# An attention and GEGLU block on Trainium2: pairs on alternating banks and longer blocks in the first max pass

## The chip, the cores and the metric

The kernel runs on one core of one Trainium2 chip. TensorE (PE) does the matrix products into PSUM, VectorE (DVE) the reductions and part of the evictions, ScalarE (ACT) the exponentials and the other evictions, GpSimd (POOL) elementwise work between tiles in SBUF, and SyncE (SP) issues most transfers. The metric is the device time of one execution in microseconds (us).

## The reference

The input x has 2048 rows of 576. After a layer norm, two branches are computed and joined:

```python
xn = layernorm(x)
qkv = (xn @ wqkv)            # 32 heads of 18
p = softmax(q @ k.T * 18 ** -0.5)
s = (p @ v) @ wo
h = gelu(xn @ w_gate) * (xn @ w_up)      # 4608 columns
g = silu(h @ w_down)
out = x + s * g
```

## The kernel before, in words

Each float32 matrix is split into two float16 parts (hi and lo), and a product is three float16 products. The heads are worked on in 16 passes of two heads, each of 64 blocks. For a pass the kernel first needs the maximum of each score row: `qk1` computes a block of 128 x 512 scores of both heads into a tile s1 or s2, and VectorE reduces it to PM (L1218, L1221). Later `qk2` computes the transposed scores, already less the maximum, and ScalarE takes the exponential (L1270, L1276). `max_end` turns the maxima of a pass into two rows of QT.

In the main loop (15 passes) the max blocks of the next pass run beside the exponential blocks of this one. For the first pass (p = 0) there is nothing before, so its 64 max blocks stand alone, filled with other work of TensorE: first the values (`unit_v`, 16 x 2 units of 14 matmuls, evicted by ScalarE to vst and stored to VS), then the stream of *pairs*. Five steps follow, with the first four max blocks of pass 1 and the transposition of the maxima; after them the main loop begins.

The pairs are the projections of the remaining heads (units j1 to j4, four pairs each) and the gate and up products of the 18 chunks c0 to c17 of 256 hidden columns (eight pairs each). A pair fills two PSUM tiles at once: `Pair.slot` issues two matmuls on 64 rows each, one for each tile. A pair has 27 slots, 14 in the first half and 13 in the second, where the two row halves change tiles; between the halves a small VectorE copy (`touch`, L414) orders them. The tiles are `MTile("ma")` and `MTile("mb")`. At the end of a j pair, `evac_j` empties them: evh by ScalarE (L490), evl by VectorE (L495), then six stores to KD and QD on SP (L510). At the end of a c pair, gs and gv are copied by ScalarE (L609, L620), GpSimd and ScalarE compute the gelu and split the result into hhi and hlo, and the down product (`down`, `DownPair`, L730) is queued in `dnq`. `g_run(n)` issues up to n slots of the stream; a half that has ended lets the next begin only with another block.

In the main loop `make_plan` deals the slots that are left (`gs.left`) over the blocks that are left, with the stages of the down pairs (12 matmuls each) and with bursts of the products with the values (L1311), which use md, ma or mb.

The weights of a unit are prepared by the pieces of `prep`: load, a maximum of each of five parts (L234) and of the two parts of the down weights (L239), exchange of the maxima through DRAM, power of two, split into hi (ScalarE) and lo (GpSimd). `subtick` moves the queue of these pieces and of deferred steps on by one tick, as far as its room of time for each engine allows. The tile raw has one buffer, so a load waits for the split of the unit before. The order of the units is v, j1, c0, c1, j2 and so on, and a unit's weights are started two units ahead.

Of the kernel before, what the change touches and what calls it, by code (L numbers as in the profile page):

```python
# [12 lines left out]
F32 = mybir.dt.float32  # L13
# [7 lines left out]
P = 128  # L21
# [12 lines left out]
FIRST = {"A": 0.75, "V": 0.75, "T": 1.3}  # L34
# [53 lines left out]
def on_dve(t=0.7):  # L88
    return {"V": t}
# [7 lines left out]
def kernel(ctx: ExitStack, tc: tile.TileContext, x, wqkv, wo, w_gate, w_up, w_down, out):  # L97
# [33 lines left out]
    defer = Deferred()  # L131
# [60 lines left out]
    class W:  # L192
        pass

    def prep(name, parts, n, down=None, urgent=False, free=None, dfree=None, lead=1, slow=1):


        w = W()
        w.ready = False
        w.n = n  # L200
        pieces = []
        gap = 0 if urgent else 1
# [135 lines left out]
        def fin():  # L338
            w.ready = True

        def add(fn, cost=None):
# [7 lines left out]
        low_cost = dve if urgent else on_pool(2.75)  # L349
        pieces += [(None, None)] * (lead * gap)  # L350
        add(load)
        rest(5 * slow)
        for t in range(5):
            add(lambda t=t: amax(t), dve)
        if down is not None:
# [41 lines left out]
    def half_terms(w, i, cs, xs, half, more):  # L397
# [9 lines left out]
            terms.append((w.lo[r, 4, i, cs], (XT, XU)[half][r, xs]))  # L407
        return terms

    def touch(ap):  # L410

        t = sm.tile([1, 2], F32, tag="touch", name="touch", bufs=2)
        o = t[:, 0:1] if len(ap.shape) == 2 else t.rearrange("p (a b) -> p a b", a=2)
        nc.vector.tensor_copy(o, ap)  # L414

    class Pair:
# [8 lines left out]
        def begin(self):  # L425
            w, ia, ib, cs, xs = self.args
            n = cs.stop - cs.start
            if self.stage == 0:
                self.a = MTile("ma", [P, 512], F32, self.end.readers)
                self.b = MTile("mb", [P, 512], F32, self.end.readers)  # L430
            a, b = self.a.t[0:n], self.b.t[0:n]
            more = self.stage == 0
            self.q = [
                ((a, b)[half ^ self.stage], half_terms(w, (ia, ib)[half ^ self.stage], cs, xs, half, more))
                for half in range(2)
            ]
            self.k = 0
            self.slots = len(self.q[0][1])
# [160 lines left out]
    def gu(w, c, sb, ft):  # L599

        st = {}
        gp = nc.gpsimd
        k = glu["n"]
        glu["n"] += 1

        def end(g, u):
            until(lambda: glu["cubic"] == k)
            st["g"] = wp.tile([P, 512], F32, tag="gs", name=f"gs_{c}_{sb}_{ft}", bufs=1)
            nc.scalar.activation(st["g"], g.t, AF.Copy, scale=w.uE[:, 0:1])  # L609
            g.done()  # L610
            defer.at(defer.now + 1, lambda: up(u), on_act())

        end.readers = 1

        def up(u):
            if glu["low"] < k - 1:
                defer.at(defer.now + 1, lambda: up(u), on_act())
                return
            st["v"] = wp.tile([P, 512], F32, tag="gv", name=f"gv_{c}_{sb}_{ft}")
            nc.scalar.activation(st["v"], u.t, AF.Copy, scale=w.uE[:, 1:2])  # L620
            u.done()
            defer.at(defer.now + 1, cubic)

        def cubic():
            if glu["hp"] < k:
                defer.at(defer.now + 1, cubic)
                return
            glu["cubic"] += 1
            defer.at(defer.now + 2, th, on_act())
            defer.spend(on_pool(4.2))  # L630
            st["t"] = wp.tile([P, 512], F32, tag="tw", name=f"tw_{c}_{sb}_{ft}", bufs=1)
            gp.tensor_tensor(st["t"], st["g"], st["g"], op=ALU.mult)  # L632
            gp.tensor_scalar(st["t"], st["t"], GC, 1.0, op0=ALU.mult, op1=ALU.add)
            gp.tensor_tensor(st["t"], st["t"], st["g"], op=ALU.mult)
            gp.tensor_tensor(st["v"], st["v"], st["g"], op=ALU.mult)

        def th():
            nc.scalar.activation(st["t"], st["t"], AF.Tanh, scale=GK)  # L638
            defer.at(defer.now + 1, hp)
            defer.at(defer.now + 2, hhi, on_act())  # L640

        def hp():
            glu["hp"] += 1
            defer.spend(on_pool(1.9))
            gp.tensor_scalar(st["t"], st["t"], 1.0, 1.0, op0=ALU.mult, op1=ALU.add)  # L645
            gp.tensor_tensor(st["v"], st["v"], st["t"], op=ALU.mult)

        def hhi():
            if ft == 0:
                if not all(k[0] < c - 1 or v.left == 0 for k, v in list(hstate.items())[:-1]):  # L650
                    defer.at(defer.now + 1, hhi, on_act())
                    return
                hs = hstate[c, sb] = W()
                hs.left = 8
                hs.hi = wp.tile([P, 2, 512], F16, tag="hhi", name=f"hhi_{c}_{sb}")
                hs.lo = wp.tile([P, 2, 512], F16, tag="hlo", name=f"hlo_{c}_{sb}")
            elif (c, sb) not in hstate:
                defer.at(defer.now + 1, hhi, on_act())
                return
            nc.scalar.activation(hstate[c, sb].hi[:, ft], st["v"], AF.Copy)  # L660
            defer.at(defer.now + 1, hlo)

        def hlo():
            glu["low"] += 1
            hs = hstate[c, sb]
            defer.spend(on_pool(1.2))
            gp.tensor_tensor(hs.lo[:, ft], st["v"], hs.hi[:, ft], op=ALU.subtract)  # L667
            if ft == 1:
                defer.at(defer.now + 1, lambda: dnq.extend(
                    (w, c, sb, si, hf) for si in range(4) for hf in range(2)  # L670
                ))

        return Pair(w, 0, 1, slice(P * ft, P * ft + P), slice(512 * sb, 512 * sb + 512), end)

    dnq = deque()
# [753 lines left out]
    load_v(0)  # L1429
    stage.open("b")  # L1430
    steps = max_end(0)
# [264 lines left out]
```

## Time and profile before

| | |
|---|---|
| median of 3 runs | 2632.76 us (2630.01 to 2633.9) |
| profiled execution | 2633.47 us, span 2631.7 us |
| granted TensorE clock, mean | 0.991 |
| first max block's reduction begins | 88.48 us |
| first exponential's scores begin | 213.71 us |
| TensorE busy | 2539.2 us |

All times inside the profile count from the start of the span. A row of the timeline has its start, its duration, the engine, the line and the operation with its shapes, and in brackets how long the engine was idle before it and what released it. A matmul's own duration (377 ns for 512 columns) is longer than the distance to the next one, since matmuls are pipelined and two on 64 rows each run side by side.

### The profile page before, as it was taken

What the parts mean: (1) busy time and instruction counts of PE and PEld (TensorE: products, weight loads), DVE (VectorE), ACT (ScalarE), POOL (GpSimd) and SP (SyncE); (2) the same over time, 40 slices, a digit from 0 to 9 for tenths busy, and PEclk for the clock granted to TensorE, in tenths of its full rate; (3) what the DMA queues carried; (4) which work ended last, traced back from release to release, by engine and by line L of the source; (5) the groups of instructions that cost most, each with busy time, mean ns of one, the idle gap of its engine ahead of it and who ended that gap; (6) DMA issues with size and microseconds to landing.
All of it is one profiled execution on the core that took longest, in us unless ns stands there. A gap on an engine that the chain in (4) does not pass through costs nothing.

```text
span 2631.7 us, 59621 instructions
## 1 busy us (share of the span) xinstructions
PE 2539.2 (96%) x25232; PEld 1316.7 (50%) x25232; DVE 1945.6 (74%) x2720; ACT 1660.8 (63%) x2083; POOL 1491.2 (57%) x1422
## 2 busy tenths in 40 slices
PE   6979999999999999999999999999999999999898
PEld 5554445445554545344545554555455555454344
DVE  7676777777787777777877777787778877777444
ACT  5216666666677666666666666777666666666563
POOL 4236654476437554567576666757576665756301
PEclk9989999999999999999999999999999999999999
DMA  4430111201130112111011111102010101100123
GB/s 144 138 90 22 29 44 31 81 18 28 45 94 12 28 38 60 36 39 54 12 43 20 37 25 39 44 22 56 9 51 15 40 23 39 49 9 11 35 77 117
DMA packets 133640, 118.61 MB, mean 45 GB/s; under 512 B 60160, under 2 KB 112792, under 8 KB 133372
## 3 DMA queue, kind: packets, MB, share of 16 engines
q1 hardware_dynamic: 127740, 103.02, 14.9%
q0 software_dynamic: 3072, 8.90, 1.0%
q8 instruction: 197, 3.23, 0.6%
q10 hardware_dynamic: 2560, 2.89, 0.3%
q14 instruction: 71, 0.58, 0.1%
HBM read 84.89 MB, written 29.61 MB: 44 GB/s over the span
## 4 chain that ended last, share of the span: by engine, by line
PE 82%; DVE 8%; ACT 4%; issue 3%; DMA 2%; POOL 1%; SPq 0%; ACTq 0%; DVEq 0%
PE mb_t L444 16%; PE ma_t L444 15%; PE md_t L730 14%; PE s L1270 8%; PE md_t L1311 8%; PE s L1218 8%; PE ma_t L1311 6%; DVE PM L1221 3%; PE pv L1292 1%; PE mc_t L463 1%; ACT P L1276 1%; PE mb_t L1311 1%; DMA obr<-rd 1%; DVE m_c L234 1%; PE mb_t L463 1%
## 5 line engine op out<-in xcount | busy, mean ns | idle before, releaser
L1221 DVE TENSOR_REDUCE PM<-s 128x2 f32<-128x1024 f32 x1024 | 1252.5, 1224 | 345.0 <-PE s L1218 337.0
L1276 ACT ACTIVATE P<-s,etab 128x1024 f32<-128x1024 f32 x896 | 996.7, 1112 | 615.8 <-PE s L1270 604.3
L444 PE MATMUL ma_t<-XHT,whi_c 64*128 64x512 f16 x1440 | 543.2, 377 | 9.5 <-ACT gs L609 5.1
L444 PE MATMUL mb_t<-XHT,whi_c 64*128 64x512 f16 x1440 | 543.0, 377 | 5.7 <-ACT gv L620 2.3
L444 PE MATMUL ma_t<-XHT,wlo_c 64*128 64x512 f16 x1296 | 488.7, 377 | 0.0
L444 PE MATMUL ma_t<-XL,whi_c 64*128 64x512 f16 x1152 | 434.5, 377 | 0.0
L444 PE MATMUL mb_t<-XL,whi_c 64*128 64x512 f16 x1152 | 434.3, 377 | 0.0
L444 PE MATMUL mb_t<-XHT,wlo_c 64*128 64x512 f16 x1152 | 434.3, 377 | 0.0
L1218 PE MATMUL s<-KT,QT 54*128 54x512 f16 x2048 | 404.6, 379 | 15.1 <-DVE PM L1221 10.1
L1270 PE MATMUL s<-QT,KT 56*128 56x512 f16 x2048 | 403.0, 380 | 7.8 <-ACT P L1276 3.1
L444 PEld LDWEIGHTS <-whi_c 64*128 64x128 f16 x5184 | 278.1, 94 | 250.3 <-issue 35.9
L730 PE MATMUL md_t<-dhi_c,hhi 64*128 64x288 f16 x2224 | 330.8, 283 | 1.6 <-DVE touch L414 1.2
L730 PE MATMUL md_t<-dhi_c,hlo 64*128 64x288 f16 x2224 | 330.5, 282 | 0.0
L730 PE MATMUL md_t<-dlo_c,hhi 64*128 64x288 f16 x2224 | 330.0, 282 | 0.0
L645 POOL TENSOR_SCALAR tw<-tw 128x512 f32<-128x512 f32 x144 | 90.4, 628 | 413.5 <-ACT tw L638 413.2
L730 PEld LDWEIGHTS <-hhi 64*128 64x128 f16 x4448 | 239.4, 94 | 130.7 <-issue 13.0
L667 POOL TENSOR_TENSOR hlo<-gv,hhi 128x512 f16<-128x512 f32 x144 | 168.7, 1172 | 214.8 <-ACT hhi L660 209.9
L1311 PE MATMUL md_t<-P,VT 128*32 128x512 f32 x2232 | 262.1, 597 | 0.3
L1270 PEld LDWEIGHTS <-KT 56*128 56x128 f16 x2048 | 124.1, 94 | 260.7 <-issue 173.5
L632 POOL TENSOR_TENSOR tw<-gs 128x512 f32<-128x512 f32 x144 | 152.0, 1055 | 172.7 <-ACT gs L609 172.4
L750 DVE SCALAR_TENSOR_TENSOR y<-md_t,c_c,y 128x576 f32<-128x576 f32 x262 | 211.1, 806 | 1.3 <-PE md_t L730 1.3
L444 PEld LDWEIGHTS <-wlo_c 64*128 64x128 f16 x2592 | 141.2, 94 | 119.4 <-issue 2.0
(262 smaller groups left out, 4098.1 us busy)
## 6 DMA issues: line engine op xcount, KB each, us to landing
draw_c<-in_B_w_down SPq DMA_DIRECT2D x18, 576.0 KB
raw_c<-in_B_w_gate SPq DMA_DIRECT2D x18, 512.0 KB
raw_c<-in_B_w_up SPq DMA_DIRECT2D x18, 512.0 KB
obr<-rd SPq DMA_DIRECT2D x30, 256.0 KB
KT<-KD SPq DMA_DIRECT2D x32, 224.0 KB
QT<-QD SPq DMA_DIRECT2D x32, 216.0 KB
VS<-vst POOLq DMA_DIRECT2D x16, 304.0 KB, 4.0
VT<-VS SPq DMA_DIRECT2D x16, 304.0 KB
```

Of the source, the lines that this page charges most:

```text
L444: nc.tensor.matmul(o, lw, xx, start=self.stage == 0 and self.k == 0, stop=self.stage == 1 and self.k == self.slots - 1, skip_group_check=True,
L463: nc.tensor.matmul(o, xx(t), ww[:, t, i, :], start=(k == 0), stop=False)
L632: gp.tensor_tensor(st["t"], st["g"], st["g"], op=ALU.mult)
L645: gp.tensor_scalar(st["t"], st["t"], 1.0, 1.0, op0=ALU.mult, op1=ALU.add)
L667: gp.tensor_tensor(hs.lo[:, ft], st["v"], hs.hi[:, ft], op=ALU.subtract)
L730: nc.tensor.matmul(self.t.t[:, hf, 0:288], a[r, ft, sl], b[r, ft, 288 * hf:288 * hf + 288], start=self.stage == 0 and k == 0, stop=self.st ...
L750: nc.vector.scalar_tensor_tensor(yy, y, w.c, yy, op0=ALU.mult, op1=ALU.add)
L1218: nc.tensor.matmul(s1[:, h], QT[p][r, P * qt:P * qt + P], KT[p][r, 512 * kb:512 * kb + 512], start=True, stop=True)
L1221: nc.vector.tensor_reduce(PM[p][:, :, qt, kb:kb + 1], s1, op=ALU.max, axis=AX.X)
L1270: nc.tensor.matmul(s2[:, h], KT[p][r, P * kt:P * kt + P], QT[p][r, 512 * qb:512 * qb + 512], start=True, stop=True)
L1276: nc.scalar.activation(pt, s2, AF.Exp, scale=ETAB[j0])
L1311: nc.tensor.matmul(t.t[qd:qd + 32, :], VT[p][:, c0:c0 + 32], pt[:, h], start=kt == k0, stop=kt == k1, skip_group_check=True,)
```

## The change

In the first max pass:

- While the values last, two max blocks are issued back to back, with twice the filling behind them.
- Behind the values, `g_run(7)` instead of `g_run(5)`, and a second, smaller `subtick` for each block.
- The pairs alternate between the banks ma, mb and the banks mc, pv, up to block 56; from there and in the main loop only ma, mb.

And in the preparation: a unit is `ready` before its down weights are split, with a flag `dready` of its own for these, on which the queueing of downs waits; c0's pieces rest 7 ticks behind the load instead of 10.

```diff
-    def prep(name, parts, n, down=None, urgent=False, free=None, dfree=None, lead=1, slow=1):
+    def prep(name, parts, n, down=None, urgent=False, free=None, dfree=None, lead=1, slow=0):
...
-        rest(5 * slow)
+        rest(5 + slow)
...
+            add(fin)
             pieces.append(Gate(dfree))
             add(lambda: dsplit_hi(0), act)
             add(lambda: dsplit_hi(1), act)
             add(lambda: dsplit_lo(0), on_pool(3.0))
             add(lambda: dsplit_lo(1), on_pool(3.0))
-        add(fin)
+            add(dfin)
+        else:
+            add(fin)
...
+    banks = deque([("ma", "mb")])
...
-                self.a = MTile("ma", [P, 512], F32, self.end.readers)
-                self.b = MTile("mb", [P, 512], F32, self.end.readers)
+                ta, tb = banks[0]
+                banks.rotate()
+                self.a = MTile(ta, [P, 512], F32, self.end.readers)
+                self.b = MTile(tb, [P, 512], F32, self.end.readers)
...
+        def queue():
+            if not w.dready:
+                defer.at(defer.now + 1, queue)
+                return
+            dnq.extend((w, c, sb, si, hf) for si in range(4) for hf in range(2))
...
-                lead=8 if i == 3 else 1, slow=2 if i == 2 else 1,
+                lead=8 if i == 3 else 1, slow=2 if i == 2 else 0,
...
-    for k in range(64):
+    k = 0
+    while k < 64:
         if k == 12:
             load_qk(1)
-        qk1(0, k)
-        subtick(FIRST)
         if done_units[0]:
-            g_run(5)
+            if k < 56 and len(banks) == 1:
+                banks.append(("mc", "pv"))
+            elif k >= 56 and len(banks) == 2:
+                banks.remove(("mc", "pv"))
+            qk1(0, k)
+            subtick(FIRST)
+            g_run(7)
+            subtick({"A": 0.75, "V": 0.3, "T": 0.5})
+            k += 1
         else:
-            fill(0.95)
+            qk1(0, k)
+            qk1(0, k + 1)
+            subtick(FIRST)
+            subtick(FIRST)
+            fill(1.9)
+            k += 2
```

What this moves is shown at three places; a name such as s_0_46 is the tile of max block 46 of pass 0, and a number behind it is only the tile's own. On TensorE, the end of the first pair of j1 and the start of the second stand so before:

```order
L444 MATMUL mb_t<-XHT,whi_j_1358 126x512
L444 LDWEIGHTS whi_j_1358
L444 MATMUL ma_t<-XHT,whi_j_1358 126x512
L1218 LDWEIGHTS QT_1074
L1218 MATMUL s_0_46_1980<-KT_1075,QT_1074 128x512 [waits DVE_49]
L1218 LDWEIGHTS QT_1074
L1218 MATMUL s_0_46_1980<-KT_1075,QT_1074 128x512
L444 LDWEIGHTS whi_j_1358
L444 MATMUL ma_t<-XHT,whi_j_1358 126x512 [waits DVE_49]
L444 LDWEIGHTS whi_j_1358
L444 MATMUL mb_t<-XHT,whi_j_1358 126x512 [waits DVE_49]
```

and so in the changed kernel:

```order
L454 MATMUL mb_t<-XHT,whi_j_1349 126x512
L454 LDWEIGHTS whi_j_1349
L454 MATMUL ma_t<-XHT,whi_j_1349 126x512
L1232 LDWEIGHTS QT_1074
L1232 MATMUL s_0_44_1979<-KT_1075,QT_1074 128x512 [waits DVE_49]
L1232 LDWEIGHTS QT_1074
L1232 MATMUL s_0_44_1979<-KT_1075,QT_1074 128x512
L454 LDWEIGHTS whi_j_1349
L454 MATMUL mc_t<-XHT,whi_j_1349 126x512 [waits Activation_49]
L454 LDWEIGHTS whi_j_1349
L454 MATMUL pv_t<-XHT,whi_j_1349 126x512 [waits Activation_49]
```

The second pair begins two blocks earlier, and on banks that the values used last instead of those of the first pair. On VectorE, the maxima of c1's weights stand before among the max blocks of pass 1:

```order
L1221 TENSOR_REDUCE PM_1080<-s_0_63_2275 128x2 [waits PE_49]
L495 SCALAR_TENSOR_TENSOR evl_1_3_2294<-ma_t,evh_1_3_2292 126x512 [waits DMAHW5_49,DVE_49,Activation_49]
...
L414 COPY touch<-mb_t 1x1 [waits PE_49]
L1221 TENSOR_REDUCE PM_1469<-s_1_2_2433 128x2 [waits PE_49]
L234 TENSOR_REDUCE m_c_2442<-raw_c_2279 128x1 [waits DMAHW6_49,DMAHW4_49]
```

and in the changed kernel in block 56 of pass 0:

```order
L505 SCALAR_TENSOR_TENSOR evl_1_3_2262<-mc_t,evh_1_3_2260 126x512 [waits DMAHW5_49,DVE_49,Activation_49]
L505 SCALAR_TENSOR_TENSOR evl_0_3_2266<-pv_t,evh_0_3_2264 126x512 [waits DMAHW7_49,Activation_49]
L1235 TENSOR_REDUCE PM_1080<-s_0_56_2268 128x2 [waits PE_49]
L234 TENSOR_REDUCE m_c_2275<-raw_c_2203 128x1 [waits DMAHW6_49,DMAHW4_49]
L1235 TENSOR_REDUCE PM_1080<-s_0_57_2297 128x2 [waits PE_49]
L234 TENSOR_REDUCE m_c_2275<-raw_c_2203 128x1
L422 COPY touch<-mb_t 1x1 [waits PE_49]
```

The maxima now stand ahead of a touch and of seven of the 64 reductions, behind the fourth j1 pair's evl. On SP, behind the third j1 pair's stores (evl_0_2 is its last), before:

```order
L510 DMA QD_1879<-evl_0_2_2199 7x18x512
L215 DMA raw_c_2279<-in_B_w_gate 128x4x256
L219 DMA raw_c_2279<-in_B_w_gate 128x1x256
L215 DMA raw_c_2279<-in_B_w_up 128x4x256
L219 DMA raw_c_2279<-in_B_w_up 128x1x256
L227 DMA draw_c_2284<-in_B_w_down 128x2x576
L1210 DMA VT_2296<-VS 128x16x38
L510 DMA KD_1880<-evh_1_3_2292 7x18x512
```

and in the changed kernel:

```order
L520 DMA QD_1882<-evl_0_2_2171 7x18x512
L215 DMA raw_c_2203<-in_B_w_gate 128x4x256
L219 DMA raw_c_2203<-in_B_w_gate 128x1x256
L215 DMA raw_c_2203<-in_B_w_up 128x4x256
L219 DMA raw_c_2203<-in_B_w_up 128x1x256
L227 DMA draw_c_2208<-in_B_w_down 128x2x576
L520 DMA KD_1883<-evh_1_3_2260 7x18x512
```

c1's load keeps its place between the third pair's stores and the fourth's; only the transfer of VT goes from before to behind the fourth pair's stores.

More of the change, by code (lines that the diff above doesn't have):

```diff
@@ L193 @@
         pass
-    def prep(name, parts, n, down=None, urgent=False, free=None, dfree=None, lead=1, slow=1):
+    def prep(name, parts, n, down=None, urgent=False, free=None, dfree=None, lead=1, slow=0):
         w = W()
-        w.ready = False
+        w.ready = w.dready = False
         w.n = n
@@ L339, in fin, with dfin @@
             w.ready = True
+        def dfin():
+            w.dready = True
         def add(fn, cost=None):
@@ L668, in hlo @@
             if ft == 1:
-                defer.at(defer.now + 1, lambda: dnq.extend(
-                    (w, c, sb, si, hf) for si in range(4) for hf in range(2)
-                ))
+                defer.at(defer.now + 1, queue)
+        def queue():
+            if not w.dready:
+                defer.at(defer.now + 1, queue)
+                return
+            dnq.extend((w, c, sb, si, hf) for si in range(4) for hf in range(2))
         return Pair(w, 0, 1, slice(P * ft, P * ft + P), slice(512 * sb, 512 * sb + 512), end)
```

## The prediction

> **What bounds the kernel now.** I began with the page's busy shares and its chain, to learn which engine sets the end.
>
> ```profile
> PE 2539.2 (96%) x25232; PEld 1316.7 (50%) x25232; DVE 1945.6 (74%) x2720; ACT 1660.8 (63%) x2083; POOL 1491.2 (57%) x1422
> PE 82%; DVE 8%; ACT 4%; issue 3%; DMA 2%; POOL 1%; SPq 0%; ACTq 0%; DVEq 0%
> ```
>
> TensorE is busy for 96% of the span and carries 82% of the chain. Its work is the same in both kernels, so only its lost time can be saved. The stretches (PE, PEld, DVE, ACT, POOL busy; granted clock; DMA) show where that time lies.
>
> ```profile
> 88.00:146.00 58.00, 56.68 (x380) 31.14 (x380) 51.63 (x53) 10.88 (x27) 14.65 (x30) 0.95 0.35 104
> 146.00:214.00 68.00, 53.99 (x387) 34.13 (x386) 43.34 (x58) 12.29 (x22) 24.66 (x21) 0.87 0.31 90
> ...
> 400.00:1000.00 600.00, 586.93 (x5894) 298.29 (x5894) 457.35 (x630) 402.58 (x522) 333.84 (x316) 1.00 0.17 42
> 1000.00:1600.00 600.00, 592.51 (x6072) 298.49 (x6072) 465.09 (x640) 402.25 (x468) 383.11 (x346) 1.00 0.15 38
> 1600.00:2200.00 600.00, 594.90 (x6170) 304.50 (x6164) 466.96 (x634) 408.85 (x529) 391.50 (x358) 1.00 0.13 33
> ...
> 2420.00:2632.00 212.00, 191.81 (x1487) 92.83 (x1481) 98.65 (x157) 107.51 (x118) 42.19 (x44) 0.95 0.22 72
> ```
>
> The second row is the rest of the first max pass behind the values, with the five steps after it. TensorE idles 14.0 of 68 us there and has 0.87 of its clock, worth up to 8.8 us more. The three long rows are the main loop: 25.7 us idle in 1800, at full clock. What TensorE waits for in the second row:
>
> ```profile
> PE ma_t L444 <- DVE evl L495: 5.2, 4, 1.5
> PE mb_t L444 <- DVE evl L495: 4.9, 4, 1.4
> ...
> PE mb_t L444 <- DVE touch L414: 1.1, 2, 0.8
> ```
>
> At the end of each pair of the unit j1 the next begins on the same two banks, and waits until ScalarE (evh) and VectorE (evl) have emptied them. TensorE's rows show one such place, and windows of 3 us the clock after it.
>
> ```profile
> 153.06 0.43 PE L1218 MATMUL s<-KT,QT 54*128 54x512 f16 x2
> ...
> 154.35 0.43 PE L1218 MATMUL s<-KT,QT 54*128 54x512 f16 x2
> ...
> 155.22 0.43 PE L1218 MATMUL s<-KT,QT 54*128 54x512 f16 x2
> 156.85 0.37 PE L444 MATMUL ma_t<-XHT,whi_j 64*126 64x512 f16 x1 [1.19 <-DVE evl L495]
> 158.58 0.51 PE L444 MATMUL mb_t<-XHT,whi_j 64*126 64x512 f16 x1 [1.35 <-DVE evl L495]
> ```
>
> ```profile
> 156.00:159.00 3.00, 0.80 (x4) 0.46 (x5) 2.47 (x4) 1.83 (x4) 2.92 (x3) 0.95 0.21 56
> 159.00:162.00 3.00, 3.00 (x18) 2.32 (x16) 0.74 (x1) 0.00 (x0) 2.92 (x3) 0.50 0.45 143
> ```
>
> A score block with five slots takes 1.29 us, with three 0.87: 0.215 for a slot and 0.215 for the block. After 0.80 us of work in 3 the clock stands at one half.
>
> **The change part by part.**
>
> *Score blocks by twos among the values (40 blocks).* The same matmuls stand in another order.
>
> ```profile
> 120.77 0.39 PE L1218 MATMUL s<-KT,QT 54*128 54x512 f16 x2
> ...
> 122.05 0.39 PE L1218 MATMUL s<-KT,QT 54*128 54x512 f16 x2
> ...
> 145.71 0.70 PE L1218 MATMUL s<-KT,QT 54*128 54x512 f16 x4
> ```
> ```profile
> L1221 DVE TENSOR_REDUCE PM<-s 128x2 f32<-128x1024 f32 x39 | 47.3, 1222 | 19.9 <-PE s L1218 19.4
> ```
>
> A block costs 1.28 us alone; two back to back cost 0.70 instead of 2 x 0.39. But VectorE must reduce each of the two tiles in 1.222 us before TensorE may refill them, so a pair cannot go far under 2 x 1.28. VectorE was busy 51.63 of 58.0 us: at most 6.4 us could go. The maxima of c0, now two at a time and two blocks earlier, may cost back up to 2 us if they meet their load. I take -0.5, between -3 and +2.
>
> *Block 40 to the first exponential's scores.* Before, this runs from 145.9 (the second half of the x4 row) to this row:
>
> ```profile
> 205.20 0.37 PE L444 MATMUL ma_t<-XHT,whi_c 64*128 64x512 f16 x1 [0.56 <-ACT gs L609]
> 205.78 0.37 PE L444 MATMUL mb_t<-XHT,whi_c 64*128 64x512 f16 x1 [0.20 <-ACT gv L620]
> ...
> 213.71 0.39 PE L1270 MATMUL s<-QT,KT 56*128 56x512 f16 x2 [1.32 <-DVE PM L1221]
> ```
>
> That is 67.8 us for six pairs (162 slots) and 28 score blocks, 190 x 0.215 = 40.9 us of work: 26.9 us are lost. The order of the changed kernel puts eight pairs (216 slots) there: 244 x 0.215 = 52.5 us. Its losses, one by one. The four j1 pairs alternate between two sets of banks, so the emptying is hidden by the 27 slots of the other pair (7 us with four blocks); what is late next is the touch between a pair's halves, which now stands behind two evl and two reductions on VectorE: I take 0.6 us each (the row above has 1.1 for two), 2.4; for two c0 pairs 0.5 each, 1.0. Three times a c0 pair follows another on the same banks: 0.56 + 0.20 as in the rows above, and with the last matmul's drain 1.3; the third has the two transfers of the maxima to QT between gs and gv on ScalarE: 2.5. Together 5.1. The last reduction costs 1.3 as before.
>
> A new wait comes with c1's weights. Their load keeps its place on SP, between the third j1 pair's stores and the fourth's, but its maxima move from behind the third max block of pass 1 into block 56, only four blocks behind the load.
>
> ```profile
> 168.50 0.74 SPq L510 DMA_DIRECT2D KD<-evh  x1
> ...
> 172.60 0.73 SPq L510 DMA_DIRECT2D QD<-evl  x1
> ...
> 185.72 0.42 SPq L215 DMA_DIRECT2D raw_c<-in_B_w_gate  x1
> ```
> ```profile
> raw_c<-in_B_w_gate SPq DMA_DIRECT2D x18, 512.0 KB
> ```
> ```profile
> 186.00:189.00 3.00, 3.00 (x18) 2.23 (x16) 1.62 (x2) 0.00 (x0) 0.00 (x0) 0.50 0.79 230
> 189.00:192.00 3.00, 2.98 (x26) 2.14 (x25) 2.51 (x4) 0.00 (x0) 0.00 (x0) 0.93 0.73 231
> ```
> ```profile
> 126.44 0.68 DVE L234 TENSOR_REDUCE m_c<-raw_c 128x1 f32<-128x512 f32 x1
> ...
> 168.64 0.68 DVE L495 SCALAR_TENSOR_TENSOR evl<-ma_t,evh 126x512 f16<-126x512 f32 x1
> ```
>
> A j1 pair takes 3 x 8 x 0.215 + 7 x 0.215 + 0.6 = 7.3 us. With block 40 at 145.4, the third pair ends at 167.3, its six stores occupy SP until 172.8 (4.8 us as above), and the first maximum needs gate and up, 1.0 MB at 230 GB/s with 0.13 MB between: 5.0 us, to about 178. The fourth pair ends at 174.6, and VectorE comes to that maximum at 177.9, after two evl and a reduction. Behind it are queued reduction 57, a second maximum and the touch, 2.5 us more, to 181.2; TensorE needs the touch at 178.4 and waits 2.8 us, 2.2 more than the usual. A wait of this length has brought the half clock above; a window of half clock as in the 159 to 162 row costs 1.7 us. I count both, 3.9. If the load came 6 us later these would be 10; if it came in time, nothing.
>
> The losses add up to 2.4 + 1.0 + 5.1 + 1.3 + 3.9 = 13.7 and the stretch to 66.2 us, 1.6 less than before, with two pairs more done.
>
> The Trainium skill (TensorE: Matmul & The Clock Gate, section "Part 1: The HAM clock gate") says that the clock falls to half after at least one idle window of about 3.4 us. By that rule the 2.8 us would bring no half clock and the sum would be 1.7 us lower; the row with 0.80 us of work in 3 had its longest gap at 1.35 us and still lost the clock, so I stay with the trace.
>
> *Splits of the down weights last.* Ready is declared before them; they are on ScalarE and GpSimd in the same order and downs wait for them by a flag of their own. c0's are done long before c0's first hidden tile, which needs two pairs and GpSimd's chain. Zero; without that cover the first down tile is later, and the plan puts slots there.
>
> *The main loop.* It gets 4067 slots instead of 4118 by the order, and two stages of down pairs fewer.
>
> ```profile
> 271.91 0.74 PE md_t L730 x12
> ...
> 97.70 1.09 PE pv_t L463 x8
> ```
>
> 51 x 0.215 + 2 x 0.74 = 12.5 us less of TensorE's work, in a loop where TensorE idles 1.4% of the time; the score blocks, exponentials and bursts stay, and VectorE (457 to 467 us of 600) and ScalarE have room. So the whole of it should come off: -12.5. The plan is dealt anew, and with 25.7 us idle in 1800 a few us either way are open: -17 to -6.
>
> *The last pass.* Two single downs of six matmuls more (6 x 1.09 / 8 = 0.8 each), three slots fewer (0.65): +1.0, between 0 and +3.
>
> **Sum** against the profiled execution (2633.47 us with what lies around its span of 2631.7): -0.5 - 1.6 - 12.5 + 1.0 = -13.6, 2619.9. The median of the runs shown, 2632.76, is 0.7 lower: 2619.2.
>
> **The rivals.**
>
> *The stretch loses less.* No wait for c1's weights and no half clock: 3.9 us less, and the touches hidden: 2.4. 2613. For it: idle never long enough elsewhere in that stretch. Against it: VectorE has four reductions and two evl (4 x 1.22 + 2 x 0.68 = 6.2 us) in each 7.3 us.
>
> *The waits come back.* The load of c1 lands 6 us later than I take, because the raw tile is free only when GpSimd has split c0:
>
> ```profile
> 163.10 1.15 POOL L324 TENSOR_TENSOR wlo_c<-raw_c,whi_c 128x512 f16<-128x512 f32 x1
> ...
> 171.53 1.28 POOL L324 TENSOR_TENSOR dlo_c<-draw_c,dhi_c 128x576 f16<-128x576 f32 x1
> ```
>
> If these stay where they are, SP is not held (172.8 against 164.3 for the weights' part), which speaks against it; the wait and a second half-clock window would make +8: 2627 to 2628.
>
> *The change does not do what it says.* The two pairs come early but the main loop doesn't shrink, because its blocks are held by VectorE or ScalarE: 2632. Against it: idle TensorE is 0.9 to 2.2% there.
>
> *Slower.* The new plan lets bursts fall right behind the pairs of j2, j3 and j4, on the bank that is still being emptied. Before, this costs little:
>
> ```profile
> PE ma_t L1311 <- DVE evl L495: 1.0, 4, 0.2
> ```
>
> At the price of the place in the first pass (1.19 + 1.35 us idle, then 1.7 by the clock: 4.2 us) four of the twelve pairs eat the gain, and from the fifth it is slower by over 0.2%: 2619.2 + 5 x 4.2 = 2640. Against it: by the order a burst on ma or mb stands behind six of the twelve pairs in both kernels.
>
> **How the numbers follow.** The forecast has 0.60, the stretch that loses less 0.14, the returned waits 0.12, no shrinking 0.07, slower 0.07. The range takes the main loop's and the stretch's bounds but not the two last rivals: 2609 to 2630. This kernel's measurement can tell 0.2%, 5.3 us, from no change: faster means under 2627.5. The returned waits lie across that bound. Faster 0.79, same 0.14, slower 0.07.
>
> **What would show it.** In the changed profile: no wait of ma or mb for evl in the first pass; the first exponential's scores at 212 +- 3 us; VectorE waiting for raw_c near 178 us, with a touch wait of about 3 us and one half-clock window behind it; TensorE idle about 1.4% in the main loop. It would be wrong if the exponentials start after 217, or if the loop from there to the last pass is not 10 us or more shorter.

## The result, and the profile after

The changed kernel takes 2631.1 us (median; 2629.17 to 2634.51) against 2632.44 us for the kernel before beside it: a ratio of 0.9999 (worked out from all executions, not from the two medians), 95% interval 0.999 to 1.0008. Nothing that can be measured was gained, where 13.6 us had been forecast. The profiled execution has a span of 2632.7 us. One of the eleven executions of the changed kernel repeated below took 6564 us and is left out of its ratio.

The first scores of the exponentials mark the start of the main loop, and those of the last pass its end. TensorE's rows of the changed kernel for both:

```profile
220.54 0.39 PE L1284 MATMUL s<-QT,KT 56*128 56x512 f16 x2 [1.32 <-DVE PM L1235]
...
2455.05 0.39 PE L1284 MATMUL s<-QT,KT 56*128 56x512 f16 x2
```

and the end of the main loop in the profile of before:

```profile
2455.02 0.39 PE L1270 MATMUL s<-QT,KT 56*128 56x512 f16 x2
```

The main loop starts 6.8 us later than before (213.71) where it should have started 2 us earlier, and lasts 2234.5 us instead of 2241.3; what follows it, the last pass, is 1.0 us longer. The same stretches as before (PE, PEld, DVE, ACT, POOL busy; granted clock; DMA):

```profile
88.00:146.00 58.00, 48.84 (x346) 29.63 (x343) 46.06 (x50) 9.99 (x25) 14.80 (x30) 0.91 0.37 108
146.00:214.00 68.00, 55.13 (x460) 35.29 (x460) 45.56 (x66) 16.37 (x28) 33.26 (x29) 0.95 0.30 87
...
400.00:1000.00 600.00, 581.43 (x5850) 299.59 (x5851) 459.49 (x635) 397.52 (x515) 326.49 (x307) 0.99 0.17 42
1000.00:1600.00 600.00, 594.68 (x6072) 296.46 (x6069) 458.73 (x631) 405.19 (x471) 383.71 (x346) 1.00 0.15 39
```

In the second row TensorE does more (460 matmuls against 387, 0.95 of the clock against 0.87), yet 12.9 of 68 us are still idle. In the third, 5.5 us more are idle than before. What TensorE waits for from 146 to 214 us, and VectorE from 88 to 214:

```profile
PE mb_t L454 <- DVE touch L422: 7.6, 3, 6.6
PE ma_t L454 <- ACT gs L619: 2.0, 3, 0.8
PE pv_t L454 <- DVE touch L422: 1.3, 2, 0.7
```
```profile
DVE mg_j L281 <- DMA mb_j<-mxd_j: 6.9, 1, 6.9
DVE m_c L234 <- DMA raw_c<-in_B_w_up: 4.6, 1, 4.6
```

The waits for evl are gone: the two sets of banks do what they should. In their place stand two waits of VectorE for transfers. The first, for j1's maxima coming back, moved out of sight in other executions (below). The second is c1's weights: SyncE's issue of the load, and VectorE's rows behind it,

```profile
176.66 0.42 SPq L215 DMA_DIRECT2D raw_c<-in_B_w_gate  x1
...
177.81 0.56 SPq L215 DMA_DIRECT2D raw_c<-in_B_w_up  x1
```
```profile
180.56 1.22 DVE L1235 TENSOR_REDUCE PM<-s 128x2 f32<-128x1024 f32 x1
186.42 0.69 DVE L234 TENSOR_REDUCE m_c<-raw_c 128x1 f32<-128x512 f32 x1 [4.64 <-DMA raw_c<-in_B_w_up]
187.03 1.22 DVE L1235 TENSOR_REDUCE PM<-s 128x2 f32<-128x1024 f32 x1
188.16 0.67 DVE L234 TENSOR_REDUCE m_c<-raw_c 128x1 f32<-128x512 f32 x1
188.75 0.14 DVE L422 COPY touch<-mb_t 1x1 f32<-1x1 f32 x1
```

and what TensorE does meanwhile, in windows of 3 and 4 us:

```profile
183.00:186.00 3.00, 0.00 (x0) 0.00 (x0) 0.00 (x0) 0.00 (x0) 0.00 (x0) 1.00 0.70 215
186.00:190.00 4.00, 1.06 (x6) 0.48 (x7) 3.58 (x6) 0.00 (x0) 0.00 (x0) 0.57 0.46 152
190.00:194.00 4.00, 4.00 (x24) 1.72 (x22) 2.04 (x4) 0.00 (x0) 0.00 (x0) 0.58 0.22 78
```

VectorE stands 4.64 us before the first maximum; the touch, on which TensorE's next half pair waits, comes at 188.75; TensorE is idle for 6.6 us and then has 0.57 and 0.58 of its clock in the windows up to 194 us. I had this wait at 2.8 us, with one window of 3 us at half clock.

### The profile page after: what moved, and what is told of

Read it like the earlier page. It is cut to its first block, busy times and chain, and to the rows that moved or that the text cites. A ratio compares the mean times of both kernels' runs of the same rounds, so it can differ in the third digit from the quotient of the medians.

```text
span 2632.7 us, 59553 instructions
## 1 busy us (share of the span) xinstructions
PE 2534.8 (96%) x25220; PEld 1317.2 (50%) x25220; DVE 1927.1 (73%) x2712; ACT 1664.6 (63%) x2083; POOL 1492.3 (57%) x1422
## 4 chain that ended last, share of the span: by engine, by line
PE 80%; DVE 9%; ACT 4%; DMA 3%; issue 2%; POOL 2%; SPq 1%; ACTq 0%; DVEq 0%; POOLq 0%
PE mb_t L454 15%; PE ma_t L454 15%; PE md_t L744 14%; PE md_t L1325 8%; PE s L1284 8%; PE s L1232 7%; PE ma_t L1325 6%; DVE PM L1235 3%; ACT P L1290 1%; PE pv L1306 1%; PE mc_t L473 1%; PE mb_t L473 1%; PE ma_t L473 1%; DVE m_c L234 1%; DMA obr<-rd 1%
## 5 line engine op out<-in xcount | busy, mean ns | idle before, releaser
L1232 PE MATMUL s<-KT,QT 54*128 54x512 f16 x2048 | 399.3, 379 | 16.5 <-DVE PM L1235 13.8
L1325 PE MATMUL md_t<-P,VT 128*32 128x512 f32 x2368 | 274.9, 596 | 0.4 <-DVE y L764 0.3
L764 DVE SCALAR_TENSOR_TENSOR y<-md_t,c_c,y 128x576 f32<-128x576 f32 x261 | 210.4, 806 | 1.0 <-PE md_t L744 1.0
```

Of the source, the lines that this page charges most:

```text
L764: nc.vector.scalar_tensor_tensor(yy, y, w.c, yy, op0=ALU.mult, op1=ALU.add)
L1232: nc.tensor.matmul(s1[:, h], QT[p][r, P * qt:P * qt + P], KT[p][r, 512 * kb:512 * kb + 512], start=True, stop=True)
L1325: nc.tensor.matmul(t.t[qd:qd + 32, :], VT[p][:, c0:c0 + 32], pt[:, h], start=kt == k0, stop=kt == k1, skip_group_check=True,)
```

## The experiments

One theory was that the first stretch fails by this wait and the main loop by stalls of its own; the rivals were that one of the change's parts (twos, seven slots) costs what another brings. The start of the main loop differs by 2.5 us between the two profiles of the changed kernel, by 3.1 between two of another and by 5.8 between the two of before, so a difference of that size between two profiles proves nothing by itself; the ratio rests on all executions of a kernel. All runs in one table; the start of the main loop and its length are from the same two rows of each profile as above. The ratio is to the kernel before on the same chip.

| kernel | median, us | ratio (95% interval) | main loop starts | its length |
|---|---|---|---|---|
| before, repeated | 2626.97 | 0.9995 (0.9986 to 1.0003) | 207.89 | 2238.63 |
| changed, repeated | 2628.59 | 1.0000 (0.9991 to 1.0009) | 218.04 | 2230.95 |
| c1's maxima early | 2631.66 | 1.0008 (0.9999 to 1.0017) | 221.20 | 2231.06 |
| c1's maxima late | 2621.22 | 0.9973 (0.9964 to 0.9983) | 207.34 | 2232.14 |
| the same, repeated | 2621.50 | 0.9959 (0.9947 to 0.9972) | 210.42 | 2232.00 |
| c1's load early | 2630.41 | 1.0002 (0.9994 to 1.0011) | 221.78 | 2232.02 |
| j1's return late | 2626.24 | 0.9999 (0.9991 to 1.0008) | 212.87 | 2233.85 |
| j1's and c1's late | 2628.56 | 1.0005 (0.9994 to 1.0015) | 207.72 | 2241.57 |
| no twos | 2628.40 | 1.0000 (0.9991 to 1.0008) | 218.00 | 2230.80 |
| one set of banks | 2629.33 | 1.0008 (0.9999 to 1.0017) | 221.08 | 2227.45 |
| one set, c1's maxima late | 2625.64 | 0.9990 (0.9981 to 0.9998) | 213.47 | 2232.74 |
| before + banks | 2622.22 | 0.9979 (0.9970 to 0.9988) | 202.03 | 2242.34 |
| before + banks + seven slots | 2627.57 | 1.0000 (0.9991 to 1.0010) | 210.19 | 2238.40 |
| c1 late + product late | 2627.69 | 0.9993 (0.9984 to 1.0002) | 209.77 | 2238.57 |
| c1 late + burst in ma | 2626.24 | 0.9985 (0.9976 to 0.9994) | 209.96 | 2237.73 |
| c1 late + both | 2630.11 | 1.0005 (0.9996 to 1.0014) | 209.49 | 2239.48 |

**The wait for c1's weights: taken away, repeated, lengthened.** On the changed kernel, the maxima later (late) or earlier (early), the load unmoved:

```diff
-                lead=8 if i == 3 else 1, slow=2 if i == 2 else 0,
+                lead=8 if i == 3 else 1, slow={2: 2, 3: 14}.get(i, 0),   # late
+                lead=8 if i == 3 else 1, slow={2: 2, 3: -3}.get(i, 0),   # early
```

Late: 

> One edit to the changed kernel: the preparation of c1 rests twelve blocks more between its load and its maxima, so that the five maxima of raw_c stand in VectorE's queue behind block 63 instead of behind block 56. Theory (the stretch from block 56 on lost 4.6 us of VectorE, 6.6 us of TensorE and some half clock because the queue stood in front of a load that took 8.5 us to land): the touch wait of 6.6 us goes, the main loop starts at 213 to 215 us instead of 220.54, total 2624 to 2627, unless c1's later weights make the main loop wait. Rival A (the stretch is slow because seven slots a block are more than VectorE and ScalarE can keep up with): the main loop still starts at 219 us or later, total 2630 or more. Rival B (the wait only moves to the first blocks of the main loop): the main loop starts early, at 213 to 215 us, but its first pass is longer by the same 5 to 7 us, total 2630 or more.

Late, repeated: 

> The kernel with c1's maxima late once more, beside the kernel with the early load, for a second profile on another chip. Theory: main loop from 206 to 210 us on, its length 2230 to 2234, ratio to before 0.996 to 0.998. Rival (the first profile caught a short first stretch): main loop from 212 us on, ratio 0.999 or more.

Early: 

> The changed kernel with the disputed wait made longer: c1's maxima three blocks earlier in VectorE's queue (behind block 54 instead of 56), its load and all else where they were. Theory (VectorE stands in front of the load and TensorE behind it): the wait before the first maximum of the up weights grows from 4 to 5 us to 7 to 9, the main loop starts 2 to 5 us later than in the changed kernel (218.0 and 220.5 us), total 2 to 5 us more. Rival (the wait is covered, and the late start has another cause): main loop and total unchanged within 1 us.

With the maxima late, TensorE's waits for a touch up to the start of the main loop at 207 us are these, and that start is the third row:

```profile
PE mb_t L454 <- DVE touch L422: 1.3, 2, 0.7
PE pv_t L454 <- DVE touch L422: 1.3, 2, 0.7
```
```profile
207.34 0.39 PE L1284 MATMUL s<-QT,KT 56*128 56x512 f16 x2 [1.32 <-DVE PM L1235]
```

The stretch runs at full clock, the loop starts at 207.3 and 210.4 us, before the forecast's 211.6 and the 213 to 215 that I expected here, and is as long as in the changed kernel: the wait is gone and has not moved. Both intervals lie below 0.9985, so this kernel beats before and, whose interval begins at 0.999, the changed one. With the maxima early VectorE's wait grows to 10.71 us and falls on a score block:

```profile
183.15 0.69 DVE L234 TENSOR_REDUCE m_c<-raw_c 128x1 f32<-128x512 f32 x1 [10.71 <-DMA raw_c<-in_B_w_up]
```

The loop starts 3.2 us later than in the repeated changed kernel, but only 0.7 later than in its first profile, and the ratio (1.0008) is not clear of 1: that less of the wait brings time is shown, that more of it costs time is not. The wait itself grew more than I expected.

**The load earlier instead.** The same place of the maxima, the load four blocks sooner:

```diff
-                lead=8 if i == 3 else 1, slow=2 if i == 2 else 0,
+                lead=4 if i == 3 else 1, slow={2: 2, 3: 4}.get(i, 0),
```

> The changed kernel with the load of c1's weights issued four blocks earlier and its maxima left behind block 56, where they are: the load now stands on SyncE's queue ahead of the stores of one j1 pair, the order on VectorE and TensorE is unchanged. Theory (VectorE stands before a load that was issued too late): the load goes out at about 169 us in place of 177 and lands by 175 to 179, the wait before the first maximum of the up weights falls from 4 to 5 us to 0 to 1, TensorE's touch wait of 7 us goes with its half clock, the main loop starts at 208 to 212 us, total 6 to 9 us below the changed kernel. Rival (the load lands late because it shares the DMA engines with the stores of the pairs, wherever it is issued): the wait stays over 3 us or the stores come late, main loop at 215 us or later.

The rival came true. VectorE no longer waits for raw_c, but ScalarE's next eviction does, for the stores that now stand behind the load, and TensorE behind both (ScalarE's row, then TensorE's):

```profile
183.72 0.60 ACT L500 ACTIVATE evh<-pv_t 126x512 f16<-126x512 f32 x1 [6.37 <-DMA KD<-evh]
```
```profile
186.23 0.61 PE L1232 MATMUL s<-KT,QT 54*128 54x512 f16 x2 [6.10 <-DVE PM L1235]
```

The load (2 x 512 + 2 x 128 + 576 = 1856 KB, by an estimate 8 to 9 us at the 202 to 241 GB/s that the changed kernel's windows from 176 to 183 us show) now holds up the stores of the pairs behind it (6 x 126 KB each). Of the places tried, only the later use frees both VectorE and ScalarE. The Trainium skill (DMA: Bandwidth & Descriptors, section "Queues, rings and completion order") says that SyncE's copies share one row of rings, each consumed in ring order. The landings that this run's trace records agree: the last ones of gate's small transfer (L219), of up's large and small one, of the down weights and of the first store behind them come in the order of issue, at 175.19, 176.67, 179.60, 181.08 and 182.18 us.

Yet the stores in front are not what makes the load long. A trace records up to 16 landings for one transfer; call each a piece. In the changed kernel, c0's load has nothing issued on SyncE for 16 us before it:

```profile
93.70 0.33 SPq L1216 DMA_DIRECT2D QT<-QD  x1
110.27 0.40 SPq L215 DMA_DIRECT2D raw_c<-in_B_w_gate  x1
```

Its last piece of up's large transfer lands 9.3 us after this issue; for c4 and c6, with nothing issued there for 14 and 12 us, it is 8.8 and 8.3 us; for c1, behind the six stores, 9.7. In c1's load the first piece comes 3.4 us after the issue at 176.66, 14 of up's 16 pieces are there at 183.55, and the last two come at 186.21 and 186.32, behind the two pieces (184.87 and 185.04) in which the 128 KB of gate's small transfer land. So it is in every load of every profile: each of up's last two pieces comes after one of those two.

**How far one program's first stretch varies.** The two kernels unedited:

Changed: 

> The changed kernel without an edit, run beside the next three and the kernel before, to tell what of its profile recurs. If the waits are in the program and not chance: VectorE stands 4 to 5 us before the maxima of c1's up weights, the main loop starts at 217 to 221 us, the three stalls of TensorE in passes 1 and 2 (2.9, 3.1 and 2.8 us at 109 and 145 us of pass 1 and 144 us of pass 2) are there again, and the time is that of before within 0.2%. The 6.9 us at j1's returned maxima may be partly chance: with the same program up to there the profile of the kernel with c1's maxima late shows 1.0 us; here 1 to 7 us, and the main loop earlier by as much as it is shorter.

Before: 

> The kernel before without an edit, beside the next three. The forecast of the first stretch was made against a profile in which the main loop started at 213.71 us. With the order of the main loop unchanged, the kernel with the banks alone came out 5.5 us below before, and its main loop started at 202.0 us; if the first stretch of before is the same from one execution to the next, that would be 11.7 us and not 5.5. Theory (before's profile caught a long first stretch; its usual start of the main loop is earlier): main loop at 206 to 211 us here, its length within 1.5 us of 2241.3, time equal to before's. Rival (213.71 us is usual): main loop at 212 to 215 us, and the missing 6 us must be sought elsewhere.

In the changed kernel the wait for c1 and the stalls of passes 1 and 2 came back (touch 7.0 us; 1.8, 3.1 and 2.8 us), the wait for j1's maxima was 0.6 us instead of 6.9: that one was mostly chance. In the kernel before, the loop starts at 207.89 us instead of 213.71, with the very same waits (the repeated kernel's, from 85 to 250 us):

```profile
PE ma_t L444 <- DVE evl L495: 5.2, 4, 1.5
PE mb_t L444 <- DVE evl L495: 4.9, 4, 1.4
```

and the windows around the first of them show what differs:

```profile
154.00:157.00 3.00, 0.70 (x5) 0.15 (x2) 2.95 (x4) 2.35 (x4) 2.92 (x3) 1.00 0.12 32
157.00:160.00 3.00, 2.75 (x26) 2.35 (x27) 1.42 (x2) 0.00 (x0) 2.92 (x3) 1.00 0.44 133
```

After 0.70 us of work in 3 the clock stays at 1.00, where 0.80 in 3 had brought 0.50 in the profile that I forecast from. The same gaps (1.19 and 1.35 us there, 1.19 and 1.36 here) cost the clock in one execution and not in the other. The Trainium skill (TensorE: Matmul & The Clock Gate, section "Part 1: The HAM clock gate") says of the rise to full clock that its window is free-running and its moment differs from run to run. This pair of profiles shows that the fall, too, differs from one execution to the next.

**The parts by themselves.**

```diff
 # before + banks: on the kernel before (and with g_run(7) for seven slots)
+                ta, tb = banks[0]
+                banks.rotate()
...
+            if k < 56 and len(banks) == 1:
+                banks.append(("mc", "pv"))
+            elif k >= 56 and len(banks) == 2:
+                banks.remove(("mc", "pv"))
             g_run(5)
 # one set of banks: these four lines taken out of the changed kernel
 # no twos: in the changed kernel
-            qk1(0, k + 1)
-            subtick(FIRST)
             subtick(FIRST)
-            fill(1.9)
-            k += 2
+            fill(0.95)
+            k += 1
```

Before + banks: 

> The kernel before, with one part of the change alone: until block 56 of the first max pass the gate and up pairs take the banks ma/mb and mc/pv in turn. Blocks stay single among the values, five slots a block, the weights become ready as before, so that the order of the main loop is that of before, slot for slot. Theory (the lost time of the first max pass before, 10.1 us of waits for the evictions and the half clock behind them, is one-bank waiting): the main loop starts 8 to 15 us earlier than 213.71, at 199 to 206 us, and as its work is unchanged the total is 2617 to 2625, better than the whole change. Rival (the time goes to the next thing in the queue, weight loads and VectorE's maxima, as in the changed kernel): the main loop starts at 208 us or later, total 2627 to 2633.

One set of banks: 

> The changed kernel without the second set of banks: pairs use ma/mb alone in the first max pass, all else as changed. Theory (the banks are the part that works: without them seven slots a block only mean that each next pair waits for the evictions of the last, 5 to 6 us a pair as in the profile of before): pair length back from 7.6 us to 11 to 13 us in blocks 40 to 60, evl waits of 5 us back, half clock in them, main loop from 228 to 236 us on, total 8 to 16 us over the changed kernel. Rival (the evictions are hidden behind the score blocks and the up and gate products anyway): main loop at 221 us as changed, total as changed within 3 us.

One set, c1's maxima late: 

> The changed kernel with c1's maxima late and without the second set of banks. The banks alone were worth 5.5 us in the kernel before, but only 3 us (main loop at 218.0 against 221.1 us) in the changed kernel, with c1's maxima waiting. Theory (the wait for c1's load hid what the banks bring: whatever TensorE gained up to block 56 it spent in front of a load that lands no earlier): without that wait the banks are worth more again, the main loop starts at 213 to 218 us instead of 207.3 to 209.5 and the total is 5 to 9 us above the kernel with c1's maxima late alone. Rival (the second banks bring 3 us whatever else): main loop at 210 to 212 us, total 2 to 4 us above it.

Before + banks + seven slots: 

> The kernel before with two parts of the change: two sets of banks and seven slots a block. Single blocks, and the preparations rest, and become ready, as before; this puts c1's maxima behind the second block of the main loop, since its load is issued later, and its main loop has the same 4067 slots as the changed kernel's. Theory (seven slots and two banks are good together where no load stands in the queue): main loop from 206 to 212 us on, its length 2229 to 2235, total 6 to 11 us below before. Rival A (seven slots a block cost the stretch more than they take out of the main loop): main loop at 214 us or later, total as before or slower. Rival B (the early end of the preparation is what shortens the main loop): main loop 2238 us or longer.

No twos: 

> The changed kernel with the score blocks among the values issued singly again, all else as changed. Theory (twos are worth next to nothing: block 40 came at 148.8 us with a long wait for j1's returned maxima, 145.9 before without it, and j1's reduction stands behind as many score reductions in both): block 40 at 145 to 149 us, total within 2 us of the changed kernel. Rival A (twos cost 3 us, since two reductions stand back to back and j1's reduction comes into the queue earlier): block 40 3 us earlier than in the changed kernel run beside it, total 3 us less. Rival B (twos gain): block 40 later by 2 us or more.

The banks alone are worth 5 to 6 us (ratio 0.9979; the start at 202.03 against 207.89). In the changed kernel they are worth at most 3 us at the start of the loop (221.08 against 218.04 and 220.54) and nothing that the time shows: here I had expected 8 to 16. What TensorE does sooner, it then waits for longer, in front of the same load: its longest wait for a touch is 7.0 us with two sets and 3.7 with one. With c1's maxima late they are worth 3 to 6 us at the start (213.47 against 207.34 and 210.42) and 4 to 8 in the time (0.9990 against 0.9973 and 0.9959), so the wait had hidden much of them. Twos do nothing: block 40's reduction ends at 147.6 us without and 147.4 with them.

Seven slots and the banks on the kernel before start the loop at 210.2 us, as expected, and then pass 0 takes 155.6 us instead of the changed kernel's 145.9. That makes its loop as long as rival B expects, but by this one stall. Pass 0 is as long (155.2) in the kernel with j1's and c1's preparations both late. The edit for j1, alone or with that for c1:

```diff
-        rest(4)
+        rest(wait)          # 10 for j1, 4 for the others
         add(top, on_dve(0.4))
```

J1's return late: 

> One edit to the changed kernel: the preparation of j1 rests ten blocks instead of four between sending its maxima round and reducing the copy that comes back (mg_j), so VectorE meets that reduction behind the tenth score reduction instead of the fourth. Theory (the V phase lost its time because VectorE stood 6.93 us in front of mb_j while TensorE, whose score banks it should have freed, ran dry and fell to half clock): the wait vanishes, block 40's scores come at about 145.5 us instead of 148.77, the main loop starts about 3 us earlier (217 to 218 us), total 2627 to 2629. Rival (issuing the score blocks by twos itself costs the V phase, since two reductions of 1.23 us then stand back to back in front of the value products): block 40 stays at 148 to 149 us and the total stays at 2630 to 2632.

Both late: 

> Both edits together: j1's returned maxima are reduced behind the tenth score block, c1's maxima behind the first blocks of the main loop. If the two transfer waits are what the first pass lost against the forecast, the gains add: main loop from 210 to 212 us on (the forecast had been 211.6), total 2621 to 2624. If the by-twos order or the seven slots cost it, the main loop starts at 216 us or later and the total stays above 2628.

In these two kernels with a pass 0 of over 155 us, c1's maxima fall behind block 1 of pass 1, and its splits into the middle of pass 0, where GpSimd's stand between the steps of the gelu. ScalarE's row and TensorE's wait (205 to 300 us) in the kernel with both late:

```profile
272.22 0.63 ACT L670 ACTIVATE hhi<-gv 128x512 f16<-128x512 f32 x1 [3.63 <-POOL gv L656]
```
```profile
PE s L1284 <- ACT P L1290: 6.2, 1, 6.2
```

The exponentials queue behind that split. Later is not safe in itself, then; right behind block 63 c1's maxima meet neither wait. Nor does later always cost: behind block 2 of pass 1, in the kernel before and with the banks alone, pass 0 takes 147.0 to 148.2 us. J1's return late starts the loop 5 us earlier than in the repeated changed kernel (block 40's reduction at 140.9 instead of 147.4), but its ratio shows none of it: what it is worth stays open, the more so as c1's maxima move with it (behind block 59 instead of 56, the longest touch wait 2.0 us).

**The main loop.** On the kernel with c1's maxima late, the two edits singly and together:

```diff
-            chained(*dma, (4, c, on_dve()), (1, d, on_act())     # product late
+            chained(*dma, (7, c, on_dve()), (1, d, on_act())
...
-                flush(("ma", "mb") if d else ("md", "ma"))        # burst in ma
+                flush(("ma", "mb") if d or 57 <= i <= 60 else ("md", "ma"))
```

Both: 

> The changed kernel with c1's maxima late (as before) and two edits to the main loop that leave its slots and blocks where they are: the multiplication of the normalisation (osb<-osb,obr) comes three blocks later, and a burst that falls on blocks 57 to 60 of a pass takes the bank ma in place of md, which the transposition of the row maxima needs next. Theory (the main loop lost 5 to 6 us of its forecast gain of 12.5 to three stalls of TensorE behind VectorE's queue in passes 1 and 2, 8.8 us with 2 to 4 us of half clock behind them): all three stalls go, the main loop is 8 to 12 us shorter than the 2232.1 us with c1's maxima late alone, 2220 to 2224 us, and the total is 9 to 12 us below that kernel's 2621.2. Rival (the plan's loss is spread over all passes, and what does not stall there stalls a few blocks on): the main loop stays within 3 us of 2232, total 2618 or more.

Product late: 

> One of the two main-loop edits alone, on the kernel with c1's maxima late: the multiplication of the normalisation three blocks later. The two together made the main loop 7 us longer instead of shorter. Theory A (the bank did it: a burst in ma is awaited by the next pair): here the stall of 1.8 to 2.9 us at 109 us of pass 1 goes and nothing new comes, main loop 2228 to 2231 us, total 1 to 4 us below the kernel it is made from. Theory B (moving the multiplication did it, since the steps behind it, the split and its stores, then fall in busier blocks): main loop 2235 us or longer.

Burst in ma: 

> The other main-loop edit alone, on the kernel with c1's maxima late: bursts of blocks 57 to 60 in the bank ma. Theory A: the stalls of 3.1 and 2.8 us at the ends of passes 1 and 2 go, but pairs wait for the burst's addition in their place, 1.5 to 2 us each in passes 1, 2 and 11, and the main loop is 2 to 7 us longer than 2232. Theory B (this edit is harmless and the multiplication is to blame): main loop 2226 to 2231 us.

The stalls that they aim at are VectorE's queue ahead of the addition that empties md (rows of the kernel with c1's maxima late, repeated; then TensorE's):

```profile
495.96 0.80 DVE L292 TENSOR_SCALAR E_c<-E_c 128x2 f32<-128x2 f32 x1
496.86 0.17 DVE L297 RECIPROCAL s_c<-E_c 128x2 f32<-128x2 f32 x1
497.06 0.92 DVE L298 TENSOR_SCALAR s_c<-s_c 128x2 f32<-128x2 f32 x1
497.90 0.68 DVE L1333 TENSOR_TENSOR osb<-md_t,osb 128x512 f32<-128x512 f32 x1
```
```profile
498.62 0.27 PE L1254 MATMUL md_t<-ident,rmc 128*64 128x128 f16 x1 [3.07 <-DVE osb L1333]
```

With the burst in ma that wait disappears and passes 1 and 2 are 4.5 us shorter together (297.8 us against 302.3), but from 225 to 2400 us these waits stand in its place, where the first had been 1.1 us and the second absent from the list:

```profile
PE ma_t L454 <- DVE osb L1333: 7.1, 15, 1.9
PE ma_t L1325 <- ACT gs L619: 6.1, 11, 2.1
```

The loop is 6 us longer. The product late costs as much, and both together 7: theories A and B were each half right. The rival of the first expectation holds in its reading, not in its bound of 3 us: what does not stall there stalls elsewhere, and these edits do not show that the loop could be shorter.

## Why the prediction was wrong, point by point

- **Score blocks by twos, -0.5.** Held within its bounds: no effect.
- **Four j1 pairs without the emptying.** Held: TensorE's waits for evl are gone, and a pair takes 7.6 us (7.3 forecast).
- **c1's weights, +3.9: the step that failed most.** Place and mechanism were right, the size was not. I let gate and up land 5.0 us after the third pair's stores were issued, counting 1.0 + 0.13 MB at 230 GB/s; it was 9.8 us (176.66 to 186.42). The stores in front explain little of that, since loads without them took 8.3 to 9.3 us (above). What bytes at a rate leave out is the 3.4 us to the first piece and the 2.7 us by which the last two pieces of up trail the others, behind gate's small transfer. The forecast had the price at hand: in the profile of before, c1's load was issued at 185.72 and its last piece of up landed at 195.25, 9.5 us later. The touch wait was 6.6 and 7.0 us instead of 2.8, and the half clock behind it covers two windows instead of one. Without the wait the start of the loop is 208.9 us in the mean of two profiles instead of 219.3: 10.4 us. The rival "the waits come back" had about this size (+8), but a wrong reason (the raw tile); the load was issued without being held.
- **The 26.9 us lost before.** A hidden step: I took the half clock of one profile for a fixed price of the gaps. The repeated kernel has the same gaps and starts the loop 5.8 us earlier, with 0.97 and 0.95 of the clock in the two stretches from 88 to 214 us instead of 0.95 and 0.87. I had asked whether the clock falls, but not how often.
- **The main loop, -12.5.** The direction held, the size only in part. Ten profiles with the changed order and neither an edit to the loop nor GpSimd's stall give 2227.5 to 2234.5 us, mean 2231.8; three with the order of before 2238.6 to 2242.3, mean 2240.8: -9.0, inside -17 to -6. That the missing 3.5 us are the three stalls of passes 1 and 2 is likely, but not shown, since taking them away cost more elsewhere.
- **The last pass, +1.0.** Held: 177.7 and 178.1 us against 176.7 and 176.3.

In the means of two profiles each, the loop starts 8.5 us later (219.3 against 210.8) instead of 2.1 earlier, is 7.2 us shorter instead of 12.5 and the last pass 1.4 longer: +2.7 in these four profiles, where the times show no change within 0.1%.

The forecast named its own refutations, and both came: exponentials after 217 us (220.5 and 218.0) and a main loop less than 10 us shorter (6.8 between the two profiles compared first). The wait for c1's weights is the largest part: with one number of the preparation changed, the kernel gains 0.3 to 0.4%. Half of that or more is the banks', which gain 0.2% alone; what the seven slots and the other parts add to them is not clear of the intervals (0.9947 to 0.9972 and 0.9964 to 0.9983 against 0.9970 to 0.9988).

## What to carry to other kernels

Before an instruction of an in-order engine is moved towards a transfer, read from a profile when that transfer's last piece lands after its issue, instead of dividing bytes by a rate, and see what the engine's queue holds behind the wait. A faster stretch ahead of a fixed arrival gains nothing; find the arrival first, and move its user rather than the transfer. And take a price from a second execution before it becomes a term of a sum: the part made of clock may not be there.

## What the hardware showed that I had not expected

- The same gaps of 1.19 and 1.35 us brought a window of half clock in one execution (0.50) and none in another (1.00); over the first stretch that was about 5.8 us.
- VectorE operations on 128 x 2 elements (L292, L298) took 0.80 and 0.92 us in the main loop where a reciprocal of the same shape took 0.17; such small steps ahead of an addition in the queue make up much of TensorE's stall of 3.07 us. It is not the operation that is slow: of the 36 in the changed kernel, the 13 beside which no GpSimd instruction ran took 0.15 to 0.17 us, the 23 with one 0.09 to 1.19, and the 18 reciprocals 0.17 either way.
- A load of gate and up (two transfers of 512 KB, each followed by one of 128 KB) had its large transfers landed 8.2 to 11.7 us after the first issue, in all 18 loads of the changed kernel.
- The exchange of j1's maxima through DRAM made VectorE wait 6.9, 0.6, 1.0 and 4.0 us in four profiles of kernels that are the same up to there.
